# Making a cross-covariance already turned: k'q in place of q'k, with the norms spread by two TensorE turns

## The chip, the cores and the metric

The kernel runs on one core of a Trainium2 chip. The metric is the device time of one execution in microseconds (us), lower is better. Executions of one kernel mostly agree within 0.3%.

Engines in the profile: PE is TensorE's matmuls, PEld its weight loads, DVE VectorE, ACT ScalarE, POOL GpSimd, SP SyncE.

## The reference, cut to what matters

```python
B, N, C = 4, 6208, 256
qn = q / (norm(q, axis=1, keepdims=True) + 1e-06)      # norms of the columns, over N
kn = k / (norm(k, axis=1, keepdims=True) + 1e-06)
s  = kn.transpose(0, 2, 1) @ qn / tau                  # (B, C, C): rows by k, columns by q
a  = softmax(s, axis=-1)                               # over q's columns
x  = v @ a                                             # (B, N, C)
# then a channel mix on x: xk, xr = mixes of x and its predecessor in the sequence
# k = relu(xk @ w_k); out = sigmoid(xr @ w_r) * (k*k @ w_v)
```

The output is float32, and the kernel works on bfloat16 operands with f32 sums.

## The kernel before: the parts that matter

The channel mix of batch b runs while q and k of a later batch are loaded, squared and multiplied into that batch's covariance. The work is cut into blocks of 512 rows of x, a block into eight steps of about 1.1 us. A batch's softmax is a list of pieces, and each step takes one off it. For batches 1 to 3:

```python
def unit_matmul(b, g, s):                       # q stationary, k moving: S has q along the partitions
    ...
    nc.tensor.matmul(s_ps[:, ih, :], rows_at(qk, b, g, 0)[:rows, s, ih * P:(ih + 1) * P],
                     rows_at(qk, b, g, 1)[:rows, s, :], ...)

def invert():                                   # rn: 1/norm of q in columns 0:2, of k in 2:4 (= rk)
    nc.vector.tensor_scalar_add(rn, rn, 1e-6)
    nc.vector.reciprocal(rn, rn)
    for h in range(2):
        nc.vector.tensor_scalar_mul(s_sb[:, h], s_sb[:, h], rn[:, h:h + 1])
    ...
def turn():                                     # four f32 turns, into PSUM
    st_ps[b] = ps.tile([P, 2, C], F32, name="st_ps", tag="xT_ps", bufs=2)
    for n in range(4):
        ...
        nc.tensor.transpose(st_ps[b][:, ih, dh * P:(dh + 1) * P], s_sb[:, dh, ih * P:(ih + 1) * P], ident_f)
def exp(halves):                                # reads st_ps, scale = k's inverse norm
    ...
return [evac, None, norms, roots, pow2, None, invert, None, None, turn,
        lambda: exp([0]), lambda: exp([1]), shares, lambda: weigh(0), lambda: weigh(1)]
```

The order within a step decides this case (condensed; `...` marks what is cut):

```python
for j in range(8):
    if j == 1 and i >= 1: finish(i - 1, 3)      # ScalarE tanh, then VectorE's output product;
    elif j % 2 and j > 1: finish(i, j // 2 - 1) #   the latter frees a vr_ps buffer (there are two)
    ...
    piece()                                     # the softmax piece of this step
    up(i + 1, j)                                # w_k product -> kT_ps, ScalarE relu -> kr
    ...square, down                             # kk = kr*kr on VectorE; w_r and w_v products -> vr_ps
    if j in (0, 2): x_half(i + 2, ...)          # a half of the next x tile: TensorE, ScalarE's copy
    ...mixes, transposes of v, a unit of covariance, sums of squares
```

## Time and profile before

| of before | |
|---|---|
| time, first three runs | 503.56 us (503.54 to 503.62) |
| span of the profiled execution | 502.1 us |
| TensorE, VectorE, ScalarE busy | 96%, 85%, 85% |
| softmax pieces of batches 1, 2, 3 | about 127 to 147, 243 to 262, 359 to 376 us |

How to read it: from 50 to 480 us TensorE has work at every moment, so the end moves with what its queue holds and with what it waits for. The lines themselves are shown in the prediction below.

### The profile page before, as it was taken

To read this page: it belongs to the slowest core of one execution; us is meant where nothing else is said; L and a number is where in the kernel's file an instruction comes from. 1 tells how busy PE (TensorE), PEld (TensorE's weight loads), DVE (VectorE), ACT (ScalarE), POOL (GpSimd) and SP (SyncE) were. 2 spreads that over 40 slices of the span, in tenths; PEclk is the share of its full clock that TensorE was granted. 3 is DMA by queue.
4 is the path that set the end of the run, shared out by engine and by line. 5 is a ranking of instruction groups with operands and counts; after the bars stand their busy time and mean duration, and the time that the engine had idled before them with its cause. 6 is when DMAs were issued, how large, how long until landed. Compare 5 with 4: busy or idle time off the path is not lost.

```text
span 502.1 us, 9301 instructions
## 1 busy us (share of the span) xinstructions
PE 481.3 (96%) x3437; PEld 331.0 (66%) x3437; DVE 428.4 (85%) x786; ACT 428.7 (85%) x872; POOL 96.6 (19%) x142
## 2 busy tenths in 40 slices
PE   1789999999999999999999999999999999999996
PEld 0355677667666766766776676676666666666675
DVE  2778899999988998998989899899898787878794
ACT  3789998999899889889998898998888888788884
POOL 0043421222333132121223323100031010000000
PEclk9999999999999999999999999999999999999999
DMA  8999999999799999997599999972296657345123
GB/s 325 418 315 197 201 193 174 211 208 199 146 184 184 200 168 180 148 196 121 139 188 154 190 175 180 177 140 64 75 198 104 152 90 153 77 107 85 58 69 106
DMA packets 131542, 83.46 MB, mean 166 GB/s; under 512 B 50532, under 2 KB 125608, under 8 KB 130472
## 3 DMA queue, kind: packets, MB, share of 16 engines
q0 software_dynamic: 55824, 33.01, 49.7%
q1 hardware_dynamic: 75352, 49.59, 40.0%
q8 instruction: 27, 0.44, 0.4%
q10 hardware_dynamic: 320, 0.26, 0.2%
q14 instruction: 19, 0.16, 0.1%
HBM read 78.71 MB, written 25.43 MB: 207 GB/s over the span
## 4 chain that ended last, share of the span: by engine, by line
PE 91%; DMA 4%; ACT 2%; DVE 1%; issue 1%; SPq 1%; ACTq 0%; DVEq 0%
PE vr_ps L596 33%; PE kT_ps L564 33%; PE vr_ps L592 8%; PE xT_ps L458 8%; PE s_ps L293 6%; DMA f<-in_k_dram 3%; ACT k L160 1%; DMA v_bf<-in_v_dram 1%; SPq L125 1%; ACT qk L155 0%; PE y_ps L636 0%; PE st_ps L353 0%; DVE k L167 0%; PE kT_ps L504 0%; DVE k L170 0%
## 5 line engine op out<-in xcount | busy, mean ns | idle before, releaser
L569 ACT ACTIVATE kr<-kT_ps 128x512 bf16<-128x512 f32 (+1 forms) x390 | 234.5, 604 | 33.2 <-PE kT_ps L564 29.5
L596 PE MATMUL vr_ps<-w_v_sb,kk 128*128 128x256 bf16 x1536 | 230.3, 273 | 0.0
L564 PE MATMUL kT_ps<-xk,w_k_sb 128*128 128x512 bf16 (+1 forms) x780 | 229.8, 377 | 0.0
L596 PEld LDWEIGHTS <-kk 128*128 128x128 bf16 x1536 | 150.3, 98 | 57.3
L577 DVE TENSOR_TENSOR kk<-kr 128x2048 bf16<-128x2048 bf16 (+1 forms) x148 | 125.6, 850 | 0.2 <-ACT kr L569 0.2
L606 DVE SCALAR_TENSOR_TENSOR res<-res,vr_ps 128x256 f32<-128x256 f32 x192 | 79.8, 416 | 50.1 <-ACT res L605 50.1
L564 PEld LDWEIGHTS <-w_k_sb 128*128 128x128 bf16 x780 | 75.5, 98 | 27.5 <-issue 0.6
L605 ACT ACTIVATE res<-vr_ps 128x256 f32<-128x256 f32 x192 | 76.5, 398 | 1.3 <-PE vr_ps L596 1.3
L592 PE MATMUL vr_ps<-w_r_sb,xr 128*128 128x256 bf16 x384 | 73.3, 273 | 0.0
L460 ACT CAST xT<-xT_ps 128x512 bf16<-128x512 f32 x94 | 55.9, 595 | 20.0 <-PE xT_ps L458 19.6
L549 DVE SCALAR_TENSOR_TENSOR xk<-delta,mu_t,xT 128x512 bf16<-128x512 bf16 x94 | 69.9, 745 | 0.0
L549 DVE SCALAR_TENSOR_TENSOR xr<-delta,mu_t,xT 128x512 bf16<-128x512 bf16 x94 | 69.9, 745 | 0.0
L592 PEld LDWEIGHTS <-xr 128*128 128x128 bf16 x384 | 37.6, 98 | 44.6 <-issue 0.2
L133 POOL DMA_DIRECT2D qk<-in_q_dram x39 | 26.1, 669 | 168.2 <-ACT kr L569 138.2
L458 PE MATMUL xT_ps<-vT,a_sb 128*128 128x512 bf16 x188 | 55.9, 379 | 0.0
L293 PE MATMUL s_ps<-qk 128*128 128x256 bf16 (+1 forms) x294 | 55.8, 273 | 0.0
L402 POOL DMA_DIRECT2D v_bf<-in_v_dram x48 | 36.6, 764 | 97.0 <-DMA vT<-v_bf 47.9
L254 ACT ACTIVATE sq<-qk 128x1024 bf16<-128x1024 bf16 x48 | 51.0, 1063 | 0.0
L199 PE MATMUL s_ps<-qk 128*128 128x384 bf16 (+2 forms) x98 | 20.0, 355 | 15.1 <-ACT qk L155 15.1
L539 DVE TENSOR_TENSOR delta<-xT 128x1024 bf16<-128x1024 bf16 x47 | 32.2, 685 | 0.7 <-ACT xT L460 0.7
L293 PEld LDWEIGHTS <-qk 128*128 128x128 bf16 (+1 forms) x294 | 28.5, 98 | 5.6 <-issue 0.8
L133 POOL DMA_DIRECT2D qk<-in_k_dram x39 | 25.9, 665 | 3.8 <-DMA w_k_sb<-in_moe_w_k_dram 2.4
(113 smaller groups left out, 249.5 us busy)
## 6 DMA issues: line engine op xcount, KB each, us to landing
out_dram<-res SPq DMA_DIRECT2D x47, 512.0 KB, 4.8
v_bf<-in_v_dram POOLq DMA_DIRECT2D x48, 256.0 KB, 7.1
qk<-in_q_dram POOLq DMA_DIRECT2D x36, 256.0 KB, 6.2
qk<-in_k_dram POOLq DMA_DIRECT2D x36, 256.0 KB, 7.8
f<-in_q_dram SPq DMA_DIRECT2D x4, 1024.0 KB, 13.4
f<-in_k_dram SPq DMA_DIRECT2D x4, 1024.0 KB, 11.0
f<-in_q_dram SPq DMA_DIRECT2D x3, 512.0 KB, 7.7
f<-in_k_dram SPq DMA_DIRECT2D x3, 512.0 KB, 6.1
```

Source lines behind the costliest of these rows:

```text
L133: nc.gpsimd.dma_start(rows_at(qk, b, g, i)[:rows, :n], qk_src(t, b, g))
L293: nc.tensor.matmul(s_ps[:, ih, :], rows_at(qk, b, g, 0)[:rows, s, ih * P:(ih + 1) * P], rows_at(qk, b, g, 1)[:rows, s, :], start=t0 and ih ...
L458: nc.tensor.matmul(xT_ps, a_sb[:, b, ih, dh * P:(dh + 1) * P], vT[:, :, ih, :], start=ih == 0, stop=ih == 1)
L460: nc.scalar.copy(xT[:, dh, 1:], xT_ps)
L549: nc.vector.scalar_tensor_tensor(o[:, dh], st[i, "d"][:, dh], mu[:, dh:dh + 1], st[i, "x"][:, dh, :M], op0=OP.mult, op1=OP.add)
L564: nc.tensor.matmul(kT_ps[:, :m], w_k_sb[:, dh, fh * P:(fh + 1) * P], xk[:, dh, :m], start=dh == 0, stop=dh == 1)
L569: nc.scalar.activation(kr, kT_ps[:, :m], AF.Relu, scale=0.5 ** 0.5)
L577: nc.vector.tensor_tensor(st[i, "kk"][:, fh // 4 * 4 + lo:fh + 1, :m], kr, kr, op=OP.mult)
L592: nc.tensor.matmul(vr_ps[:, D:], xr[:, dh, s * P:(s + 1) * P], w_r_sb[:, dh, :], start=dh == 0, stop=dh == 1)
L596: nc.tensor.matmul(vr_ps[:, :D], kk[:, fh, s * P:(s + 1) * P], w_v_sb[:, fh, :], start=fh == 0, stop=fh == 7)
L605: nc.scalar.activation(res[:, s], vr_ps[:, D:], AF.Tanh, scale=0.5)
L606: nc.vector.scalar_tensor_tensor(res[:, s], res[:, s], 1.0, vr_ps[:, :D], op0=OP.add, op1=OP.mult)
```

## The change

S is to come out with k along the partitions, as the softmax wants it, so that its 256x256 values need no turning. q's inverse norms, which stood along the partitions, must then stand along the columns: each of their two columns is repeated 128 times as a stationary operand and turned, and one VectorE product applies both.

```diff
-            nc.tensor.matmul(s_ps[:, ih, :], rows_at(qk, b, g, 0)[:rows, s, ih * P:(ih + 1) * P],
-                             rows_at(qk, b, g, 1)[:rows, s, :], ...
+            nc.tensor.matmul(s_ps[:, ih, :], rows_at(qk, b, g, 1)[:rows, s, ih * P:(ih + 1) * P],
+                             rows_at(qk, b, g, 0)[:rows, s, :], ...
 (cut)
         def invert():
             nc.vector.tensor_scalar_add(rn, rn, 1e-6)
             nc.vector.reciprocal(rn, rn)
-            for h in range(2):
-                nc.vector.tensor_scalar_mul(s_sb[:, h], s_sb[:, h], rn[:, h:h + 1])
+        def rows_of_q():
+            rq_ps[b] = ps.tile([P, C], F32, name="rq_ps", tag="xT_ps", bufs=2)
+            for h in range(2):
+                nc.tensor.transpose(rq_ps[b][:, h * P:(h + 1) * P], rn[:, h:h + 1].to_broadcast([P, P]), ident_f)
+        def spread():
+            nc.vector.tensor_tensor(s_sb, s_sb, rq_ps[b].unsqueeze(1).to_broadcast([P, 2, C]), op=OP.mult)
 (cut: exp reads s_sb for b > 0)
-        return [evac, None, norms, roots, pow2, None, invert, None, None, turn, lambda: exp([0]), lambda: exp([1]),
-                shares, lambda: weigh(0), lambda: weigh(1)]
+        return [evac, None, norms, roots, pow2, None, invert, None, rows_of_q, spread, lambda: exp([0]),
+                lambda: exp([1]), shares, lambda: weigh(0), lambda: weigh(1)]
```

Batch 0 keeps its own path.

More of the change, by code (lines that the diff above doesn't have):

```diff
@@ L78 @@
     bank = {}
+    rq_ps = {}
     st_ps = {}
@@ L292, in unit_matmul @@
         for ih in range(2):
-            nc.tensor.matmul(s_ps[:, ih, :], rows_at(qk, b, g, 0)[:rows, s, ih * P:(ih + 1) * P],
-                             rows_at(qk, b, g, 1)[:rows, s, :], start=t0 and ih == 0, stop=te,
+            nc.tensor.matmul(s_ps[:, ih, :], rows_at(qk, b, g, 1)[:rows, s, ih * P:(ih + 1) * P],
+                             rows_at(qk, b, g, 0)[:rows, s, :], start=t0 and ih == 0, stop=te,
                              skip_group_check=True)
@@ L351, in turn @@
             for n in range(4):
-                ih, dh = divmod(n, 2) if b else (n % 2, n // 2)
+                ih, dh = n % 2, n // 2
                 nc.tensor.transpose(st_ps[b][:, ih, dh * P:(dh + 1) * P], s_sb[:, dh, ih * P:(ih + 1) * P],
@@ L356, in exp @@
         def exp(halves=range(2)):
+            src = s_sb if b else st_ps[b]
             for ih in halves:
                 if not bounded:
-                    nc.vector.tensor_reduce(mx[:, ih:ih + 1], st_ps[b][:, ih], axis=AX, op=OP.max, negate=True)
+                    nc.vector.tensor_reduce(mx[:, ih:ih + 1], src[:, ih], axis=AX, op=OP.max, negate=True)
                     nc.vector.tensor_tensor(mx[:, ih:ih + 1], mx[:, ih:ih + 1], rk[:, ih:ih + 1], op=OP.mult)
-                nc.scalar.activation(e_sb[:, ih], st_ps[b][:, ih], AF.Exp, scale=rk[:, ih:ih + 1],
+                nc.scalar.activation(e_sb[:, ih], src[:, ih], AF.Exp, scale=rk[:, ih:ih + 1],
                                      bias=0.0 if bounded else mx[:, ih:ih + 1],
```

## The prediction

> **What bounds the kernel now.** I read the page from the top: busy shares first, then the 40 slices, then the chain that ended last.
>
> ```profile
> PE 481.3 (96%) x3437; PEld 331.0 (66%) x3437; DVE 428.4 (85%) x786; ACT 428.7 (85%) x872; POOL 96.6 (19%) x142
> PE   1789999999999999999999999999999999999996
> PE 91%; DMA 4%; ACT 2%; DVE 1%; issue 1%; SPq 1%; ACTq 0%; DVEq 0%
> ```
>
> TensorE is busy 481.3 of 502.1 us. What is missing lies in the first and the last slices, before the block pipeline runs and after it drains. Busy time by stretches says it sharper: TensorE has 429.96 us of the 430 us from 50 to 480. The chain that ended last is 91% TensorE, and its lines are the two big products, not the softmax. So in the steady part an instruction taken off TensorE's queue should come back one for one as time, and a microsecond taken off VectorE or ScalarE should not, unless TensorE waits for it there.
>
> The softmax pieces of batches 1 to 3 run inside that steady part, one piece per step of about 1.1 us. Their costs are in the groups by line and shape (busy us, then the mean ns of one):
>
> ```profile
> L353 PE MATMUL st_ps<-ident_f,s_sb 128*128 128x128 f32 x16 | 2.4, 273 | 0.0
> L341 DVE TENSOR_SCALAR s_sb<-s_sb,rn 128x256 f32<-128x256 f32 x6 | 2.0, 374 | 0.1
> L277 DVE TENSOR_TENSOR acc<-acc,sq 128x512 f32<-128x512 f32 x27 | 18.7, 692 | 0.9
> L361 ACT ACTIVATE e_sb<-st_ps,rn 128x256 f32<-128x256 f32 x8 | 3.8, 481 | 0.0
> ```
>
> Of the 16 turns, 12 belong to batches 1 to 3; batch 0 has its own path, which the change leaves alone. L277 matters only as a yardstick for a 128x512 f32 product.
>
> **What the Trainium skill says.** (1) "Perfetto Trace Analysis", section "Summary: the profiler window per engine type": TensorE's end is an estimate, only starts are seen. So I take TensorE's cost from the spacing of starts. In batch 1 the four turns start at 139.69 and the next matmul at 140.13: 0.44 us for four, 0.11 us each, not the 273 ns of the row. (2) "TensorE: Matmul & The Clock Gate", section "Part 4: PE-mode transpose": about 275 ns for a 128x128 turn in a kernel's context. The row's 273 agrees, as a duration, but it isn't what the queue pays. (3) "VectorE: DVE Perf Modes", section "The perf-mode tier table": f32 tensor_tensor runs at 1x and any PSUM operand holds it there, while f32 tensor_scalar in SBUF runs at 2x. The trace fits: 692 ns for a 512-wide product, against 333 to 352 ns for an undisturbed 256-wide scalar multiply. (4) The same page, section "The TRN2 errata": ScalarE pays a fixed 224 cycles from SBUF against 172 from PSUM, by which an exp from SBUF would cost some 40 ns more (estimate from that page at its 1.2 GHz). No exp of before reads SBUF, so this trace does not show it.
>
> **The change part by part.** The covariance product exchanges its operands: k is the stationary one and q the moving one. Shapes, counts and types stay (288 matmuls of 128x256 at the same pace), and S comes out with k along the partitions already, as the exp wants it. Cost: none.
>
> Removed from TensorE: four f32 turns per batch at 0.11 us, 0.44 us. Added: two f32 turns of the norms' column repeated 128 times, with the same shape as those removed. At the same 0.11 us that is 0.22 us. Net **-0.22 us per batch, -0.66 us for three**, all of it on the path that sets the end if nothing new waits. I assume that a stationary operand with step 0 loads no slower (141 ns before, hidden behind other matmuls).
>
> VectorE: removed two scalar multiplies, 0.62 to 0.76 us per batch; added one 128x512 f32 product with a PSUM operand, about 0.69 us as L277. Net about zero. It moves by two steps, from before the turns to after them.
>
> ScalarE: two exps per batch read SBUF in place of PSUM, perhaps +0.04 to +0.06 us each, under 0.4 us in all, beside TensorE's work.
>
> PSUM: both old and new tile take a slot of the pair xT_ps. The old one was held from the turns to the second exp (139.69 to 143.8 in batch 1), the new one only until the product. I found no wait for this slot before, so no gain.
>
> **The place where a wait can come in.** The list of pieces is 15 long in both versions, but the turns stood three pieces after the inversion, and the new turns stand two after it. They need the reciprocal. So TensorE reaches them one step sooner than it reached the old turns. I went through the timeline of the three batches, asking when the reciprocal is done and where TensorE's queue will stand.
>
> Batch 1: reciprocal done at 137.59 + 0.18 = 137.77; the new turns fall ahead of the matmul at 138.50. No wait.
>
> Batch 2: the turns were one piece further in the block (ahead of 254.70), so the new ones fall ahead of the matmul at 252.86, whose weights load at 252.75. Reciprocal done at 252.37 + 0.18 = 252.55. About 0.2 us of slack, just enough.
>
> Batch 3: TensorE has no covariance of a later batch to do any more, so its steps are shorter, while VectorE is still behind. The timeline:
>
> ```profile
> 367.64 0.21 PEld L564 LDWEIGHTS <-w_k_sb 128*128 128x128 bf16 x2
> 367.70 0.16 DVE L338 TENSOR_SCALAR rn<-rn 128x4 f32<-128x4 f32 x1
> 367.75 0.59 PE L564 MATMUL kT_ps<-xk,w_k_sb 128*128 128x512 bf16 x2
> 367.90 0.18 DVE L339 RECIPROCAL rn<-rn 128x4 f32<-128x4 f32 x1
> ...
> 368.73 0.59 PE L458 MATMUL xT_ps<-vT,a_sb 128*128 128x512 bf16 x2
> ...
> 369.16 0.60 PE L353 MATMUL st_ps<-ident_f,s_sb 128*128 128x128 f32 x4
> ```
>
> The columns are start, length, engine, line. The old turns sit at 369.16, well after the reciprocal. The new ones sit one step earlier, just ahead of the up-projection matmul at 367.75, and the reciprocal is done only at 367.90 + 0.18 = 368.08. Then comes the way from VectorE to TensorE (elsewhere in this trace about 0.05 us: a_sb done at 39.72, its weights load at 39.77) and a load of about 0.1 us. First turn at some 368.2 in place of 367.75: **a new wait of 0.45 us** (0.35 to 0.55). It stands on the engine that has no slack, so it counts in full.
>
> Sum: -0.66 + 0.45 = -0.21 us, or 503.56 - 0.21 = **503.35 us**.
>
> **Rivals.** First, no new wait: VectorE might reach batch 3's inversion sooner than now, or the stall might be swallowed. Then the whole -0.66 comes out, 502.9 us. For it: the chain of waits before has hardly any wait of TensorE after 50 us. Against: VectorE runs without a break from 363.97 to the inversion, and nothing in the change touches that stretch, so its place in time should hold relative to TensorE.
>
> Second, the product becomes the wait: the exps now need VectorE, and the next x tile needs the slot. Old order in batch 2: the piece that was "turn" now stands in VectorE's queue near 254.9 to 255.6, the exp ran at 256.78 and the x matmul at 256.88. In batch 3 it is 369.3 to 370.3, against 370.72 and 371.55. If VectorE were a microsecond late, ScalarE would be held, then kr and TensorE. It could cost 0.3 to 0.5 us: 503.8 us. I think the room is enough; the removed multiplies give VectorE 0.6 us back just before.
>
> Third, batch 2's thin slack closes (its first reciprocal step took 0.40 us in place of 0.16, beside GpSimd's descriptor writing), costing up to 0.3 us: 503.6 us.
>
> Fourth, shorter VectorE or ScalarE work opens the end up: they stand at 85% and TensorE does not wait for them in the steady part, so I give it nothing.
>
> **Range and chances.** The three main outcomes lie at 502.9, 503.35 and 503.8, and the runs of before spread over only 0.08 us. I take 502.7 to 503.9 for 8 in 10. A 2% change would be 10 us; all parts together touch less than 3 us of any engine, so within 2% is nearly sure.
>
> **What the profile after would show.** Right: 12 fewer f32 turns under the old line and 6 under the new, their spacing 0.11 us; steps of batches 1 and 2 shorter by 0.22 us; a gap of some 0.45 us ahead of batch 3's new turns, with VectorE's reciprocal as the releaser; the product at about 0.69 us; the exps a little longer; busy TensorE in the steady part still near 100%, as the profile's modelled ends may hide part of a wait. Wrong: no gap in batch 3 (then 502.9), or x tiles and exps waiting for the product, or a step-0 stationary load well over 141 ns, or a clock below full.

## The result, and the profile after

The changed kernel took 504.12 us (median of 6 runs, 504.06 to 505.0) against 503.59 us for the kernel before (6 runs, 503.49 to 504.2). The ratio is 1.0013, 95% interval 1.0 to 1.0026. A ratio here is the mean time of one kernel's fast runs over that of the other's of the same rounds, so it is not quite the ratio of the two medians. This interval touches 1, and that of the repetition below includes it, so the times alone do not show a loss; the traces do. By the medians the predicted -0.21 us had the sign wrong, and the range, up to 503.9, missed the result by 0.2 us.

In the page after, the same code stands 1 to 8 lines further down (L592 is now L600, L606 is L614, L569 is L577). From the head of the page and from the chain that ended last:

```profile
PE 478.2 (95%) x3371; PEld 330.3 (66%) x3431; DVE 428.8 (85%) x783; ACT 428.4 (85%) x872; POOL 96.5 (19%) x142
PE 89%; DMA 3%; DVE 3%; ACT 2%; issue 1%; SPq 1%; ACTq 0%; DVEq 0%
```

The weight loads fell by 6 (3437 to 3431), the 12 turns less and 6 more that the diff says; the matmul count fell by 66, so 60 matmul records are missing here and busy PE can't be compared. What is new is that VectorE holds 3% of the chain that ended last, where it held 1%, so I looked for a place where TensorE now waits for it.

To find where, I took the starts of TensorE's weight loads, which are complete, and laid those of the same instruction in both traces side by side. The shift (after less before, negative is earlier):

| stretch | shift at its start | at its end | gained or lost in it |
|---|---|---|---|
| start, to 120 us | 0 | -0.26 | -0.26 |
| batch 1's softmax | -0.27 | -0.48 | -0.22 |
| batch 2's | -0.48 | -0.55 | -0.22 and +0.15 |
| batch 3's | -0.55 | +0.21 | -0.22, +0.43 and +0.55 |
| from there to 480 us | +0.20 | +0.21 | 0 |

Between the softmaxes the shift stands still to 0.01 us. The first row is chance, as the repetitions below show; from 120 us on the changed kernel **loses 0.47 us**: three times the gain of 0.22 us, less 1.13 us in three places, of which the largest two lie in batch 3. Both can be read in the timeline of the kernel after (start, length, engine, line; in brackets, how long the engine was idle and who released it). First the place that the prediction had named, where TensorE's preceding work ended at about 367.20:

```profile
367.34 0.18 DVE L340 RECIPROCAL rn<-rn 128x4 f32<-128x4 f32 x1
367.57 0.19 PEld L347 LDWEIGHTS rq_ps<-ident_f,rn 128*128 128x128 f32 x2 [0.50 <-DVE rn L340]
367.57 0.43 PE L347 MATMUL rq_ps<-ident_f,rn 128*128 128x128 f32 x2 [0.22 <-DVE rn L340]
```

The reciprocal is done at 367.52, the load of the repeated column starts 0.05 us later. The idle figures of the two TensorE rows differ because the ends are modelled; the shift of the next w_k product, from -0.56 to +0.09, gives the wait: 0.65 less the 0.22 us of the two turns is 0.43. Some three steps on comes the place that I had dismissed:

```profile
370.36 0.42 DVE L614 SCALAR_TENSOR_TENSOR res<-res,vr_ps 128x256 f32<-128x256 f32 x1 [0.66 <-ACT res L613]
370.70 0.68 DVE L350 TENSOR_TENSOR s_sb<-s_sb,rq_ps 128x512 f32<-128x512 f32 x1
...
371.41 0.51 ACT L369 ACTIVATE e_sb<-s_sb,rn 128x256 f32<-128x256 f32 x1 [0.60 <-DVE s_sb L350]
...
372.39 0.58 ACT L468 CAST xT<-xT_ps 128x512 bf16<-128x512 f32 x1
...
376.56 0.38 PE L600 MATMUL vr_ps<-w_r_sb,xr 128*128 128x256 bf16 x2 [0.63 <-DVE res L614]
```

VectorE's product stands in its queue behind an output product (L614), which itself waits for ScalarE's tanh. ScalarE's first exp waits 0.60 us for the product. In the kernel before, the same places were:

```profile
370.72 0.47 ACT L361 ACTIVATE e_sb<-st_ps,rn 128x256 f32<-128x256 f32 x1
...
372.18 0.59 ACT L460 CAST xT<-xT_ps 128x512 bf16<-128x512 f32 x1 [0.38 <-PE xT_ps L458]
...
373.09 0.42 DVE L606 SCALAR_TENSOR_TENSOR res<-res,vr_ps 128x256 f32<-128x256 f32 x1 [1.18 <-ACT res L605]
...
375.89 0.41 DVE L606 SCALAR_TENSOR_TENSOR res<-res,vr_ps 128x256 f32<-128x256 f32 x1
...
376.35 0.38 PE L592 MATMUL vr_ps<-w_r_sb,xr 128*128 128x256 bf16 x2
```

The exp starts 0.69 us later than before. ScalarE's break of 0.38 us ahead of the x tile's copy takes up most of that: the copy starts 0.21 us later (372.18 to 372.39). (The bracket counts from the end of the row before, while ScalarE's rows without a break overlap by about 0.1 us, so 0.48 us can go.) After it there is no break left. The next tanh hands the delay to VectorE's output product (373.09, now 373.29), and from there VectorE has no break until the output product of 376.09, which frees a vr_ps buffer 0.20 us later than before. TensorE had come 0.34 us ahead by then, so it waits the sum, about 0.55 us. In the kernel before, the buffer was freed at 376.30 and used at 376.35. **There was no slack** here, though no view reported a wait. The chain that ended last, in order of time (start, us, what), shows the whole path through the changed kernel's batch 3:

```profile
367.34 0.19 DVE rn L340
...
367.57 0.43 PE rq_ps L347 x2
...
369.45 0.59 ACT xT L468
370.04 0.29 ACT res L613
...
370.36 0.42 DVE res L614
370.78 0.61 DVE s_sb L350
...
371.41 0.60 ACT e_sb L369 x2
372.01 0.48 ACT kr L577
...
372.97 0.29 ACT res L613
...
373.29 0.42 DVE res L614
...
374.39 1.12 DVE kk L585
375.51 0.66 DVE xk L557
376.17 0.34 DVE res L614
...
376.56 0.38 PE vr_ps L600 x2
```

The two waits are links of one path. The turns' wait delays the x tile, the tanh behind it, and with them the product.

### The profile page after: what moved, and what is told of

It is laid out like the page before. It is cut to its first block, busy times and chain, and to the rows that moved or that the text cites. A ratio compares the mean times of both kernels' runs of the same rounds, so it can differ in the third digit from the quotient of the medians.

```text
span 502.3 us, 9227 instructions
## 1 busy us (share of the span) xinstructions
PE 478.2 (95%) x3371; PEld 330.3 (66%) x3431; DVE 428.8 (85%) x783; ACT 428.4 (85%) x872; POOL 96.5 (19%) x142
## 4 chain that ended last, share of the span: by engine, by line
PE 89%; DMA 3%; DVE 3%; ACT 2%; issue 1%; SPq 1%; ACTq 0%; DVEq 0%
PE vr_ps L604 33%; PE kT_ps L572 30%; PE vr_ps L600 10%; PE xT_ps L466 8%; PE s_ps L294 6%; DMA f<-in_k_dram 3%; ACT k L161 1%; PE s_ps L200 1%; SPq L126 1%; DVE kk L585 0%; ACT qk L156 0%; DVE xk L557 0%; DVE res L614 0%; PE y_ps L644 0%; DVE k L168 0%
## 5 line engine op out<-in xcount | busy, mean ns | idle before, releaser
L577 ACT ACTIVATE kr<-kT_ps 128x512 bf16<-128x512 f32 (+1 forms) x390 | 234.6, 604 | 33.9 <-PE kT_ps L572 29.0
L572 PE MATMUL kT_ps<-xk,w_k_sb 128*128 128x512 bf16 (+1 forms) x721 | 217.1, 377 | 0.0
L614 DVE SCALAR_TENSOR_TENSOR res<-res,vr_ps 128x256 f32<-128x256 f32 x192 | 80.1, 417 | 50.6 <-ACT res L613 50.6
L600 PE MATMUL vr_ps<-w_r_sb,xr 128*128 128x256 bf16 x384 | 73.3, 273 | 3.4 <-DVE res L614 0.6
L600 PEld LDWEIGHTS <-xr 128*128 128x128 bf16 x384 | 37.6, 98 | 45.3 <-issue 1.2
```

The lines of the kernel that those rows point to most:

```text
L572: nc.tensor.matmul(kT_ps[:, :m], w_k_sb[:, dh, fh * P:(fh + 1) * P], xk[:, dh, :m], start=dh == 0, stop=dh == 1)
L577: nc.scalar.activation(kr, kT_ps[:, :m], AF.Relu, scale=0.5 ** 0.5)
L600: nc.tensor.matmul(vr_ps[:, D:], xr[:, dh, s * P:(s + 1) * P], w_r_sb[:, dh, :], start=dh == 0, stop=dh == 1)
L614: nc.vector.scalar_tensor_tensor(res[:, s], res[:, s], 1.0, vr_ps[:, :D], op0=OP.add, op1=OP.mult)
```

## The experiments

**Theory.** The six turns less gain 0.22 us per batch as sized, and two waits eat it: A, TensorE for the reciprocal, since the turns stand one step sooner than the old ones; B, ScalarE's first exp for the product, since that stands behind an output product. **Rivals.** The exchange of the operands costs; the exps from SBUF cost; or it is chance.

All results in one table. The shift is that of TensorE's weight loads between 120 and 480 us against the first profile of before, so it is free of the start. e_swap_alone and f_exp_sbuf keep the order of the kernel before, so their 0.00 and +0.01 us also show how well the shift repeats. Times are compared only with before's (503.99 us, 11 runs, for the first four; 504.18 us, 9 runs, on another chip, for the last four).

| run | shift | batch 1 | batch 2 | batch 3 | median, us | ratio to before (95%) |
|---|---|---|---|---|---|---|
| the change, first profile | +0.47 | -0.22 | -0.07 | +0.76 | 504.12 | 1.0013 (1.0 to 1.0026) |
| a_again | +0.46 | -0.23 | -0.07 | +0.75 | 504.21 | 1.0002 (0.9988 to 1.0016) |
| c_turns_later | -0.33 | -0.22 | -0.21 | +0.11 | 503.47 | 0.9988 (0.9974 to 1.0003) |
| b_product_sooner | -0.07 | -0.22 | -0.07 | +0.22 | 503.92 | 0.9999 (0.9983 to 1.0016) |
| d_both | -0.44 | -0.22 | -0.06 | -0.15 | 503.69 | 0.9996 (0.9979 to 1.0012) |
| h_step_end | -0.65 | -0.22 | -0.22 | -0.22 | 503.10 | 0.9979 (0.9967 to 0.9992) |
| e_swap_alone | 0.00 | 0 | 0 | 0 | 503.76 | 0.9992 (0.9978 to 1.0006) |
| f_exp_sbuf | +0.01 | 0 | 0 | 0 | 503.97 | 0.9997 (0.9981 to 1.0012) |
| g_turns_sooner | +3.22 | +0.56 | +0.93 | +1.73 | 507.27 | 1.0059 (1.0046 to 1.0073) |

**The change again (a_again).**

> The changed kernel again, unaltered, to have it on the same chip as the next three. All theories: about 0.5 us over the kernel before (0.3 to 0.7). In its trace, by the starts of TensorE's weight loads against the kernel before: -0.22 us in batch 1, -0.22 then +0.15 in batch 2, and in batch 3 +0.43 ahead of the repeated turns and +0.55 near 376. The shift before the first softmax piece (-0.27 us in the first profile) should differ from profile to profile, if it is the start's chance.

The stretches repeat to 0.02 us. The shift of the first x tile after the start was -0.27 us in the first profile and -0.25 here, but this execution lost another 0.26 us between 60 and 120 us. Over all profiles the shift at 120 us lay between -0.30 and +1.41 us. The largest was in b_product_sooner, whose TensorE waited 2.0 us for the first tile of v, against 0.8 in the kernel before: that is the chance in the times. Even so the time came out 0.22 us over the kernel before, below what I had expected, because before's own runs of that call were slower (503.5 to 506.15).

**The turns later (c_turns_later).** Takes wait A away.

```diff
-        invert, None, rows_of_q, spread,
+        invert, None, None, lambda: (rows_of_q(), spread()),
```

> The repeated turns one piece later, in the old turns' place; the product stays where it is. Theory (two new waits in batch 3: TensorE for the reciprocal, 0.43 us; ScalarE's first exp for the product, which stands behind an output product in VectorE's queue, 0.60 us, passed on to TensorE as 0.55 us near 376): the first wait goes, the exp still waits 0.5 to 0.7 us, TensorE's later wait shrinks to some 0.3 us. Time 0.5 to 0.8 us under the changed kernel. Rival (the loss is exp reading SBUF, or chance of the start): no wait matters, same time as the changed kernel within 0.2 us.

As the theory said: the wait at the turns is gone, the exp still waits, and a part of the later wait is left: 0.32 us by the shift (the row's idle figure, 0.19, counts from a modelled end). Time 0.74 us under the changed kernel, shift 0.79 us under it.

```profile
369.62 0.42 DVE L614 SCALAR_TENSOR_TENSOR res<-res,vr_ps 128x256 f32<-128x256 f32 x1
369.95 0.68 DVE L350 TENSOR_TENSOR s_sb<-s_sb,rq_ps 128x512 f32<-128x512 f32 x1
370.67 0.51 ACT L369 ACTIVATE e_sb<-s_sb,rn 128x256 f32<-128x256 f32 x1 [0.59 <-DVE s_sb L350]
...
375.81 0.38 PE L600 MATMUL vr_ps<-w_r_sb,xr 128*128 128x256 bf16 x2 [0.19 <-DVE res L614]
```

Batch 2 kept its whole 0.22 us, which I had not foreseen: the +0.15 is gone as well.

**The product sooner (b_product_sooner).** Takes wait B away and leaves A.

```diff
-        invert, None, rows_of_q, spread,
+        invert, None, lambda: (rows_of_q(), spread()), None,
```

> The product one piece sooner, in the same piece as the repeated turns, which stay; so it stands ahead of the output product in VectorE's queue. Theory: the turns still wait 0.43 us for the reciprocal in batch 3, but the first exp no longer waits for the product and TensorE's wait of 0.55 us near 376 is gone or under 0.15. Time 0.4 to 0.6 us under the changed kernel. Rival: same time within 0.2 us.

The turns wait as before, the product stands ahead of the tanh-bound output product, and the exp no longer waits for it:

```profile
369.25 0.43 PE L347 MATMUL rq_ps<-ident_f,rn 128*128 128x128 f32 x2 [0.21 <-DVE rn L340]
...
370.02 0.68 DVE L350 TENSOR_TENSOR s_sb<-s_sb,rq_ps 128x512 f32<-128x512 f32 x1
...
372.36 0.52 ACT L369 ACTIVATE e_sb<-s_sb,rn 128x256 f32<-128x256 f32 x1
```

Batch 3's balance is +0.22 us, which is -0.22 for the turns and +0.44 for wait A, with nothing left near 376. The shift lies 0.54 us under the changed kernel's. The median lies only 0.29 us under that of a_again, outside the expected 0.4 to 0.6: its runs spread from 503.46 to 505.21, and the profiled one, the 505.21, had the late start.

**Both (d_both).**

```diff
-        pow2, None, invert, None, rows_of_q, spread,
+        pow2, invert, None, None, lambda: (rows_of_q(), spread()), None,
```

> Inversion one piece sooner, and the product in the same piece as the repeated turns: both waits taken away, the work is the same. Theory: no wait at the turns and none for the product; about 0.8 to 1.0 us under the changed kernel, 0.3 to 0.55 us under the kernel before. The 0.15 us in batch 2 (ScalarE's row of work) may stay. Rival (exp from SBUF or the exchange of operands costs): still slower than the kernel before.

No wait at the turns, none for the product. Shift -0.44 us, 0.90 us under the changed kernel's, as expected. The times show less of it: the median is 0.30 us under before's, but 0.52 us under a_again's where 0.8 to 1.0 was expected. Batch 2's 0.15 us stayed, and 0.07 us in batch 3 that I did not explain.

**The turns and the product at the end of the step (h_step_end).** c_turns_later had shown that batch 2 loses nothing when the turns follow the x tile's half. So this version puts both behind that half, but still ahead of the next step's output product.

```diff
-        invert, None, rows_of_q, spread,
+        invert, None, lambda: (rows_of_q, spread), None,
 (in the step)
-                if piece is not None:
-                    piece()
+                late[:] = (piece() or ()) if piece is not None else ()
 (after the x tile's half)
+            while late:
+                late.pop(0)()
```

> The turns in the old turns' place (after the x tile's first half) and the product right behind them at the end of the same step, so ahead of the output product in VectorE's queue; from the kernel with the turns later it differs in this exchange of two VectorE instructions alone (in batches 2 and 3). Theory: batch 3's exp no longer waits, TensorE's wait near 376 (0.32 us left there with the turns later) goes, batch 2 keeps no loss. Between the start and the end, by TensorE's weight loads: -0.55 to -0.66 us against the kernel before, that is the whole gain of six turns; time some 0.5 to 0.7 us under the kernel before. Rival (something besides the two waits costs in batch 3): no better than -0.35 us.

Against c_turns_later the order of VectorE's instructions differs in one exchange, in batches 2 and 3 each:

```
-L614 res<-res,vr_ps 128x256
 L350 s_sb<-s_sb,rq_ps 128x512
+L614 res<-res,vr_ps 128x256
```

That exchange is worth 0.33 us in batch 3: the exp waits 0.16 us, and TensorE's wait near 376 is gone.

```profile
369.60 0.68 DVE L350 TENSOR_TENSOR s_sb<-s_sb,rq_ps 128x512 f32<-128x512 f32 x1
370.19 0.42 DVE L614 SCALAR_TENSOR_TENSOR res<-res,vr_ps 128x256 f32<-128x256 f32 x1
370.31 0.51 ACT L369 ACTIVATE e_sb<-s_sb,rn 128x256 f32<-128x256 f32 x1 [0.16 <-DVE s_sb L350]
```

Every batch now keeps its 0.22 us. The kernel **beats the one before**: 503.10 us against 504.18 in the same rounds. Its interval, 0.9967 to 0.9992, excludes 1, though the difference is a tenth of the 2% by which kernels are called faster. Of the 1.08 us between the medians, more than the expected 0.5 to 0.7, the trace accounts for 0.65; the rest I put down to the starts, not to the change, which is not shown.

**The operands exchanged alone (e_swap_alone).** The kernel before with only the matmul's two operands exchanged. Its softmax is then wrong. (The comparison with the reference is not sharp enough to tell such an S from the right one.)

> The kernel before with k and q exchanged in the covariance products alone; wrong result on purpose (the softmax is left as it was). Theory: no cost, the trace's shift between 60 us and 480 us within 0.1 us. Rival (the exchange of the stationary operand costs): up to 0.5 us over the length of the batches.

Shift 0.00 us over all 294 products. This rival falls.

**The exps from SBUF alone (f_exp_sbuf).** The kernel before, with the exps of batches 1 to 3 reading `s_sb`; also wrong.

> The kernel before, but the exps of batches 1 to 3 read the untransposed tile in SBUF in place of the transposed one in PSUM; the turns are still done, wrong result on purpose. Theory: the exp row goes from 0.48 to 0.52 us, the trace's shift over the whole run is +0.0 to +0.2 us (ScalarE is back to back after the first exp and the place near 376 has no slack). Rival (reading SBUF is the main loss): +0.5 us or more.

An exp took 510 ns (median of six) against 478 from PSUM, and the shift is +0.01 us. This rival falls too. The reason given in the expectation, ScalarE back to back after the first exp, does not hold for the kernel before: its break of 0.38 us takes up the first exp's 0.03 us, and the second exp comes behind the tanh through which the delay of the changed kernel went.

**The turns sooner still (g_turns_sooner).** More of the suspected wait.

```diff
-        invert, None, rows_of_q, spread,
+        invert, rows_of_q, None, spread,
```

> The changed kernel with the repeated turns one piece sooner still; more of the suspected wait. Theory: a wait is the end of the reciprocal less the place of the turns in TensorE's queue, so the turns wait about 0.8 us in batch 1, 1.0 us in batch 2 and 1.4 us in batch 3, less what later waits give back (at most 0.7 us in all): 2.0 to 2.9 us over the changed kernel. Rival (the wait is hidden by other engines' slack): under 1 us.

The shift grew by 2.75 us over the changed kernel's, inside the expected 2.0 to 2.9, and the time to 507.27 us. The three waits, from TensorE's own wait list (engine, line, who, us in total, times, longest):

```profile
PEld rq_ps L347 <- DVE rn L340: 3.4, 3, 1.5
```

In the changed kernel this list has 0.5 us. So a wait of TensorE in this stretch goes into the time almost one for one (2.9 us more of it, 2.75 us in the shift).

## Why the prediction was wrong

- **TensorE bounds the steady part, and turns come back one for one.** Right. The shift is -0.22 us in each batch, -0.66 in all, to the hundredth; h_step_end kept 0.65 of it.
- **The cost of the exchange: none.** Right: 0.00 us alone.
- **A stationary operand with step 0 loads no slower.** Right: 133 to 137 ns, against 140 to 143.
- **VectorE's balance about zero.** Right: the product took 680 ns (692 from L277 was the estimate). The undisturbed multiplies of before took 333 to 355 ns, not "333 to 352". And the work moved by three pieces, not "two steps": the multiplies were in the 7th piece of the list, the product is in the 10th.
- **No wait at the turns in batches 1 and 2, one of 0.45 us in batch 3.** Right: 0.43 us, at the predicted place and with the predicted releaser, so the first rival, no new wait, did not come about. (The terms as written, 368.08 and 0.05 and 0.1 less 367.75, add up to 0.48.)
- **The second rival, "the product becomes the wait".** Here the prediction failed. It put the product in batch 3 at "369.3 to 370.3, against 370.72 and 371.55" and judged that "the room is enough". The step that failed is the product's place in VectorE's queue: those times put it right behind the output product of 369.24. But an odd step, as this one is, calls `finish` ahead of its softmax piece, so the product stands behind the next output product, that of 370.84 in the kernel before, and through it behind ScalarE's tanh. It ran at 370.70 to 371.38, and the exp waited 0.60 us, of which TensorE paid 0.55 near 376. The rival's size, 0.3 to 0.5 us, was about what it cost (0.33 us between c_turns_later and h_step_end, 0.54 between the changed kernel and b_product_sooner); what was wrong was to set it against wait A as another outcome. They are links of one path and came together: 0.43 + 0.55.
- **The slack near 376.** The prediction did not look there at all. Before's buffer was freed 0.05 us ahead of its use, and behind the x tile's copy neither ScalarE (to the next tanh) nor VectorE (from 373.29 on) has a break. That is why what was left of the exp's delay after the break of 0.38 us reached TensorE.
- **The third rival, batch 2.** The thin slack at the turns held. But 0.15 us was lost later, at a vr_ps wait of the same kind near 261.5. It goes away when the turns follow the x tile's half (c_turns_later, h_step_end) and stays where they precede it (all others with turns at their sooner place). My reading is that the turns then delay that half, and ScalarE's unbroken row behind it, by 0.2 us, up to the tanh for which VectorE's output product of 258.27 waits; that this is the carrier was argued from the trace, not tested alone.
- **The fourth rival, shorter VectorE or ScalarE work.** Not put to a test: both are as busy as before (428.8 against 428.4 us, 428.4 against 428.7). **The exps from SBUF.** Right that they cost nothing: +0.01 us. An exp grew by 32 ns (510 against 478), where some 40 were estimated.
- **The sum.** -0.66 + 0.43 + 0.55 + 0.15 = +0.47 us, against the predicted -0.66 + 0.45 = -0.21. The range leaned on three separate outcomes and left out their sum. It also leaned on a spread of 0.08 us in three runs of the kernel before, while six of them lay between 503.49 and 504.2.

## What to carry to other kernels

On an engine without slack, taking instructions away is worth just their spacing, and moving an instruction one step ahead in the queue can cost more than that. For each moved instruction, write down what stands directly ahead of it in its engine's queue, in program order, and what that in turn waits for. A view without waits doesn't mean slack: look for buffers freed just before they are used, and add up waits that lie on one path rather than treat them as alternatives. A break of an engine further down the path takes up part of a delay, so look for those too.

## What the Trainium skill lacked or had wrong

- "TensorE: Matmul & The Clock Gate", "Part 4: PE-mode transpose", gives a turn's duration (about 275 ns in context, in a passage on bf16; 273 here, f32), but not what f32 turns cost in a full queue: those of 128x128 stood 0.11 us apart, and 6 less were worth 0.65 us in all. It also has nothing on an f32 stationary operand with step 0: a column repeated 128 times loaded in 133 to 137 ns, a plain f32 one in 140 to 143.
- "Perfetto Trace Analysis", "Summary: the profiler window per engine type", marks the spread of a semaphore as hidden from the profile and gives, in that section, no figure for the way from VectorE to TensorE; here a weight load started 0.05 us after the reciprocal's end (367.52 to 367.57).
